# One row of a product order changed: the second set of unit 0 in a retention, MoE and Mish kernel

## The chip, the cores and the metric

The kernel runs on one core of one Trainium2 chip. What is measured is the device time of one execution in microseconds (us); three runs were taken of the kernel before the change. TensorE (PE) does the matrix products into PSUM, VectorE (DVE) and GpSimd (POOL) do elementwise work, ScalarE (ACT) copies and applies functions, SyncE (SP) issues most of the transfers. Each engine takes its instructions in the order in which the program hands them over, and an instruction that waits holds up everything behind it on that engine.

## The reference

Three layers in a row, on 2 x 576 = 1152 tokens of width 512:

```python
ret = scale * (q @ k.T) * Dmat          # 8 heads of 64, gamma ** (i - j) below the diagonal
x   = ret @ v                           # (1152, 512)
p   = probs / (probs.sum(-1) + 1e-9)
x   = sum over e of p[:, e] * (relu(x @ w1[e]) @ w2[e])    # 4 experts, 512 -> 1024 -> 512
h   = x @ w_in                          # 512 -> 2048
out = (h * tanh(softplus(h))) @ w_out   # 2048 -> 512
```

## The kernel before

The retention comes first (to about 37 us). Then come twelve *units* of 512 hidden columns: units 0 to 7 are the four experts (two units each), 8 to 11 the last layer. Every product is done with operands that are split into a high part, which ACT makes with a copy, and a low part, which is the rest and is made by a subtraction on DVE or POOL.

A unit's first layer, for 1024 of the tokens, is done in two *sets* of 256 hidden columns, written `("S", u, c)`. A set is a Strassen-like scheme: seven products, numbered 1 to 7, of six matmuls of 128x512 each, into four PSUM banks, one for each quarter of the result; a quarter is a token half t and a column half j. Products 1, 5, 7 and 6 open the banks of (t, j) = (0, 0), (1, 0), (0, 1) and (1, 1). Products 2, 3 and 4 add onto the banks of 1, 5 and 7. Before a bank is added onto, what it holds has to be kept: ACT copies products 1, 5 and 7 to the tiles p1, p5 and p7 (line 253).

`first_pair` (lines 639 to 694) writes the set out. `order` gives the products' order, `sum_at` the product behind which POOL adds p7 and p1 to p5. The lines that matter:

```python
                p16 = sum_tile("p16", ph); add(p16, done[n], p1)   # n == 6, L664-665
                    add(done[3], done[3], p16)          # n == 2, L669, only where 3 came earlier
            if n == sum_at:
                pool.tensor_tensor(out=p5, in0=p5, in1=p7, op=ALU.add)   # L673
                pool.tensor_tensor(out=p5, in0=p5, in1=p1, op=ALU.add)   # L674
            if n == 7:
                while later:
                    later.pop(0)()                      # weight work, handed over here
            ...
        add(done[6], done[6], p5)                       # after the last product
        hidden_high(*h6); hidden_low(*h4); hidden_low(*h6)   # h3 here too, where 3 was last
```

`add` runs on DVE (L645). The finished quarters are named after the products that end them: h2 is (0, 0), h3 (1, 0), h4 (0, 1) and h6 (1, 1). For each, `hidden_high` is the relu on ACT (L587) and `hidden_low` the low part on DVE (L596). The list `later` holds weight work: for the set ("S", 0, 1) these are two tasks, `task(pool, pool)`. The first splits the next unit's first weight chunk (ACT L175, then four subtractions on POOL, L179); the second is a set of four sums of weights on POOL (L139 to L142).

After the two sets of unit 0 the second layer begins: blocks `("Y", u, c, tb)`, 24 matmuls each (L753), for token half tb. The first block of unit 0 takes twelve matmuls with the hidden columns of set 0, then twelve with those of set 1: three with h2, three with h4, and again three and three. The first matmul of each three reads the low part. The second block reads the same hidden columns. Then comes the first set of unit 1.

Set 0 of unit 0 is written out another way (`first_plain`), since not all its operands exist yet. While it runs, DVE and ACT make the last of them: T3, T2 and T4 are differences (DVE L792) that are split (ACT L801, DVE L798). T4 is read by product 4 of the second set alone. The split's ACT copy for T4 is handed over ahead of the second set's copies p1, p5 and p7.

What the loop hands over for each set stands here:

Of the kernel before, what the change touches and what calls it, by code (L numbers as in the profile page):

```python
# [82 lines left out]
def retention_moe_mish(ctx: ExitStack, tc: tile.TileContext, kq_in, kv_in, probs, w1, w2, w64, cdec, out):  # L83
# [10 lines left out]
    order = [("O", 0, 0), ("O", 0, 1), ("G", 0, 1)]  # L94
# [97 lines left out]
    def weight_task(i, lo_engine, defer=False):  # L192
        if n_task[0] >= len(tasks):
            return
        sums, (m, u, c) = tasks[n_task[0]]
        raw = source.get(m, m), u, c
        if raw not in raw_t or not (sums or splits((m, u, c), i) and sums_at.get((m, u, c), -99) <= i - 1):
            return
        if sums:
            sums_at[m, u, c] = i  # L200
        n_task[0] += 1
        weight_sums((m, u, c)) if sums else split_w((m, u, c), lo_engine, defer)
# [14 lines left out]
    def split_x(out, src, lo_engine):  # L217
        act.activation(out=out[:, 0], in_=src, func=AF.Copy)
        lo_engine.tensor_tensor(out=out[:, 1], in0=src, in1=f32(out[:, 0]), op=ALU.subtract)
# [291 lines left out]
    def load64():  # L511
        i = n_ld[0]
        if i >= len(halves):
            return
        n_ld[0] += 1
        (m, u, c), half = halves[i]
        t = wraw.tile([P, 2, 256, 2], U32, tag="w64", name="w64", bufs=2)
        src = w64[0 if m == "O" else 1, u - NE, c, :, 2 * half:2 * half + 2]
        sp.dma_start(out=t, in_=src.bitcast(U32).rearrange("p k (n t) -> p k n t", t=2))
        raw64[i] = t  # L520
# [82 lines left out]
    def hidden(*args):  # L603
        hidden_high(*args)
        hidden_low(*args)

    def first_plain(u, c, behind):

        o = [[bank(t, j) for j in range(2)] for t in range(2)]
        h = [h_tile(u, c, i) for i in range(2)]  # L610
        for i, n in enumerate(PLAIN):
            t, j, opens = n[-3:]
            product(u, c, n, o)
            for f in behind.get(i, ()):
                f()
            if not opens:
                hidden(u, h[t][:, :, j], o[t][j])
# [94 lines left out]
    def first_last(u, c):  # L712

        o, w = ps_tile()[:, 0, :256], w_t["O", u, c]
        for k in range(4):
            for n, (a, b) in enumerate(((0, 1), (0, 0), (1, 0))):
                pe.matmul(o, xc[:, b, k], w[:, a, k], start=k == 0 and n == 0, stop=k == 3 and n == 2)  # L717
        turn_blocks(hs.rearrange("p k t -> p (k t)")[:, c * 256:(c + 1) * 256], o)
        if c == 1:
            turn_rest(hs)  # L720

    def first_last_both(u):

        n = [(2 * u + c) % 3 for c in range(2)]
        low, high = sorted(n)
        w = o_slots[:, low:high + 1:high - low]
        o = ps_tile()[:, 0]
        for k in range(4):
            for i, (a, b) in enumerate(((0, 1), (0, 0), (1, 0))):
                pe.matmul(  # L730
                    o.rearrange("p (c n) -> p c n", c=2), xc[:, b, k], w[:, :, a, k],
                    start=k == 0 and i == 0, stop=k == 3 and i == 2,
                )
        to = hs.rearrange("p k t -> p (k t)")
        if n[0] < n[1]:
            turn_blocks(to, o)
        else:
            for c in range(2):
                turn_blocks(to[:, c * 256:(c + 1) * 256], o[:, (1 - c) * 256:(2 - c) * 256])
        turn_rest(hs)  # L740
# [33 lines left out]
    def load_pb(e, tb):  # L774
        if e < E:
            pb = ph.tile([P, TB], F32, tag=f"pb{tb}", name="pb", bufs=1)
            row = p_dram[e:e + 1, tb * TB:(tb + 1) * TB]
            sp.dma_start(out=pb, in_=row.to_broadcast([P, TB]))
            pb_t[e, tb] = pb
# [5 lines left out]
    def t_first(n):  # L785
        out, x, y = {T1: (b11, b12, b11), T3: (b12, b22, b12), T2: (b11, b22, b11), T4: (b21, b21, b11)}[n]
        x_minus(out, x, y)
        hi(n, out)
        return lambda: lo(n, out)
# [174 lines left out]
    def feed_forward():  # L964
        for tb in range(NTB):
            load_pb(0, tb)
        rests = [t_first(T1), t_first(T3)]
        rests[0]()

        def first_t():  # L970
            rests.append(t_first(T2))
            rests[1]()


        sp.dma_start(out=p_last, in_=p_dram[:, NTB * TB:].rearrange("e t -> t e"))
        load64()
        load64()
        pbs = []
        i_x = seq.index(("Y", NE - 1, 0, 0))

        for i, (m, u, *at) in enumerate(seq):
            def task(*engines):
                for lo_engine in engines or (pool,):
                    weight_task(i, lo_engine)

            if m == "S":
                c, = at
                late = (u, c) in ((0, 0), (NE, 0))
                behind, order, sum_at = {}, (1, 5, 7, 6, 2, 4, 3), 7
                if (u, c) == (0, 0):  # L990
                    behind = {3: [first_t], 5: [lambda: first_last(u, 0)]}
                elif (u, c) == (0, 1):
                    behind = {1: rests[3:]}
                if (u, c) == (NE - 1, 1):
                    behind = {6: [lambda: first_last_both(u)]}
                if (u, c) == (NE, 0):
                    behind = {1: [lambda: split_x(xc, acc_last, pool)], 5: [last_x], 7: [last_t]}
                    behind[6] = [lambda: first_last(u, 0)]
                    order, sum_at = (1, 5, 7, 3, 6, 2, 4), 2
                elif (u, c) == (0, 1):  # L1000
                    later.append(lambda: task(pool, pool))
                elif (u, c) == (NE, 1):
                    later.append(lambda: task(pool, dve, dve))
                elif (u, c) == (NE + 1, 0):
                    later.append(task)
                elif c == 1:
                    later.append(lambda: task(*(pool,) * (2 if u == NE + 1 else 1)))
                if (u, c) == (0, 0):
                    first_plain(u, c, behind)
                    rests[2]()  # L1010
                    task(pool, pool)
                    rests.append(t_first(T4))
                else:
                    first_pair(u, c, behind, later, order, sum_at)
            elif m == "L":
                if u in (0, NE):
                    first_last(u, *at)
                elif at[0] == 1 and u != NE - 1:
                    first_last_both(u)
                if (u, *at) == (NU - 1, 0):  # L1020
                    for f in last_operands(u)[1:]:
                        f(T1)
            elif m == "T":
                m2_t(u)
            elif m == "V":
                last_second(u)
            else:
                if seq[i if u == NE - 1 else i - 1] == ("Y", u, 0, 0):
                    hidden(u, hl, hs)
                if i == i_x:  # L1030
                    task()
                m2(u, *at)
                if u < NE and u % 2 == 1 and at[0] == 1:
                    pbs.append((u // 2 + 1, at[1], i))

            ahead = i + 1 < len(seq) and seq[i + 1][0] == "S"

            catch_up = {("Y", 0, 0, 0): (dve, dve), ("L", 1, 0): (dve,), ("Y", 0, 0, 1): (pool, pool)}
            catch_up |= {("Y", NU - 2, 0, 1): (pool, pool)}
            catch_up |= {("Y", NE, 0, 0): (dve, pool), ("L", NE + 1, 0): (pool, pool)}  # L1040
            put_off = seq[i] in (("L", 0, 1), ("Y", NE, 0, 1), ("Y", NE, 1, 1))
            if m != "S" and i != i_x and not i_x + 2 <= i <= i_x + 4 and not put_off:
                task(*catch_up.get(seq[i], ()))
            if m != "S":
                new = (m, *at) in (("L", 0), ("L", 1), ("Y", 0, 0), ("Y", 0, 1)) and not i_x - 1 <= i <= i_x + 7 and i > 2
                turn64(new, later.append if ahead else lambda f: f())

            if not i_x <= i <= i_x + 1:
                load_w()
            if pbs and pbs[0][2] <= i - 2:  # L1050
                load_pb(*pbs.pop(0)[:2])

    feed_forward()


# [60 lines left out]
```

## Time and profile before

| What | us |
|---|---|
| Runs of the kernel before, median of 3 | 599.76 |
| Lowest and highest of them | 599.61, 599.93 |
| The profiled execution, its own time | 600.2 |
| Its span in the trace | 598.3 |
| TensorE busy in it | 590.7 (99%) |
| VectorE, GpSimd, ScalarE busy | 442.0, 394.0, 318.0 |

Busy shares are an average over stages with different limits; the stretch around the change is from 51 to 73 us, and the rows below are mostly from there. An idle time in brackets in a row is the time the engine stood still before that instruction, with what released it. A row with x8 stands for eight instructions, from the first one's start; its second number is the time from there to the last one's end.

### The profile page before, as it was taken

To read this page: it belongs to the slowest core of one execution; us is meant where nothing else is said; L and a number is where in the kernel's file an instruction comes from. 1 tells how busy PE (TensorE), PEld (TensorE's weight loads), DVE (VectorE), ACT (ScalarE), POOL (GpSimd) and SP (SyncE) were. 2 spreads that over 40 slices of the span, in tenths; PEclk is the share of its full clock that TensorE was granted. 3 is DMA by queue.
4 is the path that set the end of the run, shared out by engine and by line. 5 is a ranking of instruction groups with operands and counts; after the bars stand their busy time and mean duration, and the time that the engine had idled before them with its cause. 6 is when DMAs were issued, how large, how long until landed. Compare 5 with 4: busy or idle time off the path is not lost.

```text
span 598.3 us, 8362 instructions
## 1 busy us (share of the span) xinstructions
PE 590.7 (99%) x3069; PEld 491.7 (82%) x3069; DVE 442.0 (74%) x584; ACT 318.0 (53%) x485; POOL 394.0 (66%) x445
## 2 busy tenths in 40 slices
PE   8999999999999999999999999999999999999997
PEld 7888888888888888888888888888888888888886
DVE  4788678789779769869869859868767766245295
ACT  3566357456456455556546545425657755445360
POOL 2387759758748838847846856772787874853932
PEclk9999999999999999999999999999999999999999
DMA  8952306434623623631732632622222341220023
GB/s 326 397 184 75 109 15 192 142 89 147 188 89 94 206 88 89 213 121 53 211 121 74 220 100 86 176 80 61 56 85 88 125 124 70 71 70 1 0 72 123
DMA packets 57777, 72.29 MB, mean 121 GB/s; under 512 B 31240, under 2 KB 39048, under 8 KB 57736
## 3 DMA queue, kind: packets, MB, share of 16 engines
q1 hardware_dynamic: 57592, 71.46, 38.4%
q8 instruction: 24, 0.39, 0.3%
q10 hardware_dynamic: 144, 0.29, 0.2%
q14 instruction: 17, 0.14, 0.1%
HBM read 57.57 MB, written 14.17 MB: 120 GB/s over the span
## 4 chain that ended last, share of the span: by engine, by line
PE 90%; DMA 5%; POOL 2%; DVE 2%; ACT 1%; issue 1%; POOLq 0%; ACTq 0%; DVEq 0%; SPq 0%
PE ps L753 40%; PE b L242 38%; PE b L766 5%; PE ps L730 5%; DMA kq<-kq_in 3%; DMA cst_sb<-cdec 2%; PE ps L242 1%; POOL o L179 1%; DVE acc L792 1%; DVE x L798 1%; PE b L959 0%; PE ps L717 0%; DVE h L596 0%; ACT x L801 0%; POOL wr L142 0%
## 5 line engine op out<-in xcount | busy, mean ns | idle before, releaser
L753 PE MATMUL ps<-h,w 128*128 128x512 f32 x1056 | 243.2, 389 | 0.0
L753 PEld LDWEIGHTS ps<-h,w 128*128 128x128 f32 x1056 | 198.2, 188 | 41.4 <-DVE h L601 0.3
L179 POOL TENSOR_TENSOR w<-wr,w 128x256 fp32r<-128x256 f32 x180 | 148.0, 855 | 52.3 <-ACT w L175 52.3
L242 PE MATMUL b<-x,w 128*128 128x512 f32 x576 | 138.6, 390 | 0.0
L242 PEld LDWEIGHTS b<-x,w 128*128 128x128 f32 x576 | 107.6, 188 | 23.3 <-DVE acc L851 1.2
L179 POOL TENSOR_TENSOR o<-wr,o 128x256 fp32r<-128x256 f32 x92 | 80.4, 904 | 61.8 <-ACT o L175 61.8
L242 PE MATMUL b<-x,o 128*128 128x512 f32 x468 | 114.6, 390 | 0.6 <-ACT p L253 0.6
L242 PEld LDWEIGHTS b<-x,o 128*128 128x128 f32 x468 | 87.4, 188 | 19.3 <-ACT p L253 1.0
L645 DVE TENSOR_TENSOR b<-b,p 128x512 f32<-128x512 f32 x69 | 46.1, 695 | 34.9 <-PE b L242 32.4
L253 ACT ACTIVATE p<-b 128x512 f32<-128x512 f32 x69 | 40.4, 596 | 51.8 <-PE b L242 51.8
L175 ACT ACTIVATE w<-wr 128x1024 fp32r<-128x1024 f32 x48 | 50.3, 1054 | 28.5 <-POOL wr L142 20.6
L587 ACT ACTIVATE h<-b 128x512 fp32r<-128x512 f32 x64 | 37.8, 597 | 43.6 <-DVE b L645 32.3
L827 DVE TENSOR_TENSOR ps<-ps,pb 128x1024 f32<-128x1024 f32 x28 | 34.4, 1227 | 24.0 <-PE ps L753 24.0
L673 POOL TENSOR_TENSOR p<-p,p 128x512 f32<-128x512 f32 x23 | 33.5, 1458 | 20.5 <-ACT p L253 20.5
L540 ACT ACTIVATE e<-e,cbias 128x512 uint32<-128x512 uint32 x32 | 23.0, 718 | 42.3 <-DVE e L528 42.3
L596 DVE SCALAR_TENSOR_TENSOR h<-b,h 128x512 fp32r<-128x512 f32 x64 | 40.9, 681 | 0.0
L645 DVE TENSOR_TENSOR p<-b,p 128x512 f32<-128x512 f32 x23 | 15.8, 686 | 27.8 <-PE b L242 22.5
L551 DVE SCALAR_TENSOR_TENSOR g<-w,g 128x512 f32<-128x512 uint32 x32 | 35.9, 1123 | 0.0
L554 DVE TENSOR_TENSOR g<-g,e 128x512 f32<-128x512 f32 x32 | 34.4, 1075 | 1.1
L828 DVE TENSOR_TENSOR acc<-acc,ps 128x1024 f32<-128x1024 f32 x28 | 34.2, 1222 | 1.0
L674 POOL TENSOR_TENSOR p<-p,p 128x512 f32<-128x512 f32 x23 | 31.9, 1388 | 1.8
L766 PE MATMUL b<-w,hl 128*128 128x512 f32 x132 | 31.7, 389 | 0.0
(117 smaller groups left out, 700.1 us busy)
## 6 DMA issues: line engine op xcount, KB each, us to landing
wr<-w SPq DMA_DIRECT2D x32, 512.0 KB, 5.3
w<-w SPq DMA_DIRECT2D x32, 512.0 KB, 4.3
O<-g SPq DMA_DIRECT2D x16, 256.0 KB, 5.5
W<-g SPq DMA_DIRECT2D x16, 256.0 KB, 3.3
wr<-O SPq DMA_DIRECT2D x8, 512.0 KB, 3.8
wr<-W SPq DMA_DIRECT2D x8, 512.0 KB, 3.7
kq<-kq_in SPq DMA_DIRECT2D x7, 576.0 KB, 9.0
kv<-kv_in SPq DMA_DIRECT2D x7, 544.0 KB, 9.4
```

Source lines behind the costliest of these rows:

```text
L175: act.activation(out=w[:, 0], in_=t, func=AF.Copy)
L179: lo_engine.tensor_tensor(out=w[:, 1, k], in0=t[:, k], in1=f32(w[:, 0, k]), op=ALU.subtract)
L242: pe.matmul(o[t][j], w[:, a, 2 * kh + kk, fb * P:(fb + 1) * P], x[:, b, kk], start=opens and i == 0, stop=i == 5, skip_group_check=not opens,)
L253: act.activation(out=t, in_=src, func=AF.Copy)
L551: dve.scalar_tensor_tensor(out=g, in0=lo_w, scalar=2.0 ** -52, in1=g, op0=ALU.mult, op1=ALU.add)
L554: dve.tensor_tensor(out=g, in0=g, in1=e.bitcast(F32), op=ALU.mult)
L587: act.activation(out=out[:, 0], in_=src, func=AF.Relu)
L596: dve.scalar_tensor_tensor(out=out[:, 1], in0=src, scalar=0.0, in1=f32(out[:, 0]), op0=ALU.max, op1=ALU.subtract)
L645: dve.tensor_tensor(out=out, in0=a, in1=b, op=ALU.add)
L753: pe.matmul(o[:, j], w[:, a, d:d + P], h[:, b, f], start=i == f == n == 0, stop=i == f == 1 and n == 2,)
L766: pe.matmul(o, hl[:, a, 2 * k + f], w[:, b, f * DM:(f + 1) * DM], start=k == f == i == 0, stop=k == f == 1 and i == 2,)
L827: dve.tensor_tensor(out=o, in0=o, in1=pbb, op=ALU.mult)
```

## The change

One line is added: the second set of unit 0 gets the order 1, 5, 7, 3, 6, 2, 4 and the sums on POOL behind product 2, which only the first set of unit 8 had before. The order there was 1, 5, 7, 6, 2, 4, 3, with the sums behind product 7.

```diff
                 elif (u, c) == (0, 1):
                     behind = {1: rests[3:]}
+                    order, sum_at = (1, 5, 7, 3, 6, 2, 4), 2
                 if (u, c) == (NE - 1, 1):
```

It moves instructions on three engines. On TensorE, in the second set of unit 0, from product 7 to the second layer's first matmuls (b_804 is the bank of products 1 and 2, b_806 of 5 and 3, b_805 of 7 and 4, b_807 of 6):

```order
 L242 MATMUL b_805<-x,w 128x512 x6
+L242 MATMUL b_806<-x,w 128x512 x6
 L242 MATMUL b_807<-x,w 128x512 x6
 L242 MATMUL b_804<-x,o 128x512 x6
 L242 MATMUL b_805<-x,o 128x512 x6
-L242 MATMUL b_806<-x,w 128x512 x6
 L753 MATMUL ps<-h,w 128x512 x48
```

Product 3 has come forward from the end to the fourth place, and product 4 is now the last.

On POOL, at the same set (p_825 is p5, p_833 p7, p_816 p1; the rows on o are the first task of `later`, those on wr its second):

```order
+L179 TENSOR_TENSOR o<-wr,o 128x256 x4
+L139 TENSOR_TENSOR wr<-wr 128x2x128
+L140 TENSOR_TENSOR wr<-wr 128x2x128
+L141 TENSOR_TENSOR wr<-wr 128x2x128
+L142 TENSOR_TENSOR wr<-wr 128x2x128
 L673 TENSOR_TENSOR p_825<-p_825,p_833 128x512
 L674 TENSOR_TENSOR p_825<-p_825,p_816 128x512
-L179 TENSOR_TENSOR o<-wr,o 128x256 x4
-L139 TENSOR_TENSOR wr<-wr 128x2x128
-L140 TENSOR_TENSOR wr<-wr 128x2x128
-L141 TENSOR_TENSOR wr<-wr 128x2x128
-L142 TENSOR_TENSOR wr<-wr 128x2x128
```

The two sums into p5 now stand behind the eight instructions of the weight work, where they stood ahead of them.

On DVE, the end of the same set (p_852 and p_856 are p16; h<-b_805 is the low part of h4, h<-b_806 that of h3):

```order
-L645 TENSOR_TENSOR p_852<-b_807,p_816 128x512
-L645 TENSOR_TENSOR b_805<-b_805,p_852 128x512
+L645 TENSOR_TENSOR p_856<-b_807,p_816 128x512
+L645 TENSOR_TENSOR b_806<-b_806,p_856 128x512
 L596 SCALAR_TENSOR_TENSOR h<-b_804,h 128x512
-L645 TENSOR_TENSOR b_806<-b_806,p_852 128x512
+L645 TENSOR_TENSOR b_805<-b_805,p_856 128x512
+L596 SCALAR_TENSOR_TENSOR h<-b_806,h 128x512
 L645 TENSOR_TENSOR b_807<-b_807,p_825 128x512
 L596 SCALAR_TENSOR_TENSOR h<-b_805,h 128x512
-L596 SCALAR_TENSOR_TENSOR h<-b_806,h 128x512
 L596 SCALAR_TENSOR_TENSOR h<-b_807,h 128x512
```

The low part of h3 has moved ahead of the sum with p5 (b_807 and p_825); the low part of h4 stands right behind that sum in both. On ACT the relu of h3 now stands ahead of that of h4.

## Rows read from the trace of the kernel before

**Rows 1.** The page: busy time by engine, and the chain by engine.
```profile
PE 590.7 (99%) x3069; PEld 491.7 (82%) x3069; DVE 442.0 (74%) x584; ACT 318.0 (53%) x485; POOL 394.0 (66%) x445
...
PE 90%; DMA 5%; POOL 2%; DVE 2%; ACT 1%; issue 1%; POOLq 0%; ACTq 0%; DVEq 0%; SPq 0%
```

**Rows 2.** Chain of waits, 50 to 75 us: start, length, what.
```profile
54.56 1.69 DVE acc L792
56.25 0.02 issue
56.27 1.06 ACT x L801
57.34 0.49 ACT p L253
57.83 0.04 issue
57.87 4.37 PE b L242 x18
62.25 10.90 PE ps L753 x48
```

**Rows 3.** Timeline of TensorE: start, length, line, operation, tiles, count, idle before.
```profile
51.64 1.55 PE L242 MATMUL b<-x,o 128*128 128x512 f32 x6
53.03 4.24 PE L242 MATMUL b<-x,w 128*128 128x512 f32 x18
57.87 3.01 PE L242 MATMUL b<-x,o 128*128 128x512 f32 x12 [0.60 <-ACT p L253]
60.73 1.52 PE L242 MATMUL b<-x,w 128*128 128x512 f32 x6
62.08 11.06 PE L753 MATMUL ps<-h,w 128*128 128x512 f32 x48
72.98 1.52 PE L242 MATMUL b<-x,o 128*128 128x512 f32 x6
```

**Rows 4.** Timeline of ScalarE, around the three copies.
```profile
56.27 1.06 ACT L801 ACTIVATE x<-acc 128x1024 fp32r<-128x1024 f32 x1 [2.66 <-DVE acc L792]
57.24 1.55 ACT L253 ACTIVATE p<-b 128x512 f32<-128x512 f32 x3
58.67 1.07 ACT L175 ACTIVATE o<-wr 128x1024 fp32r<-128x1024 f32 x1
```

**Rows 5.** Line 253, 57.9 to 58.9 us: min/median/max ns, first and last start.
```profile
L253 ACT ACTIVATE p<-b x2: 590/595/600, 57.7 to 58.2; 128x512 f32<-128x512 f32 x2
```

**Rows 6.** Timeline of GpSimd, 52 to 75 us.
```profile
52.74 8.56 POOL L179 TENSOR_TENSOR w<-wr,w 128x256 fp32r<-128x256 f32 x8 [3.46 <-ACT w L175]
61.26 1.29 POOL L673 TENSOR_TENSOR p<-p,p 128x512 f32<-128x512 f32 x1
62.63 1.29 POOL L674 TENSOR_TENSOR p<-p,p 128x512 f32<-128x512 f32 x1
63.88 2.84 POOL L179 TENSOR_TENSOR o<-wr,o 128x256 fp32r<-128x256 f32 x4
66.80 0.74 POOL L139 TENSOR_TENSOR wr<-wr 128x256 f32<-128x256 f32 x1
...
69.24 0.74 POOL L142 TENSOR_TENSOR wr<-wr 128x256 f32<-128x256 f32 x1
73.55 0.85 POOL L139 TENSOR_TENSOR wr<-wr 128x256 f32<-128x256 f32 x1 [3.57 <-DVE o L179]
```

**Rows 7.** Timeline of VectorE, 63 to 73 us.
```profile
63.95 0.70 DVE L645 TENSOR_TENSOR b<-b,p 128x512 f32<-128x512 f32 x1 [0.97 <-POOL p L674]
64.56 1.88 DVE L596 SCALAR_TENSOR_TENSOR h<-b,h 128x512 fp32r<-128x512 f32 x3
67.75 1.23 DVE L825 TENSOR_TENSOR acc<-ps,pb 128x1024 f32<-128x1024 f32 x1 [1.31 <-PE ps L753]
71.11 1.22 DVE L179 TENSOR_TENSOR w<-wr,w 128x1024 fp32r<-128x1024 f32 x1 [2.14 <-ACT w L175]
```

**Rows 8.** Waits of TensorE's weight loads, 60 to 598 us: total, times, longest.
```profile
PEld b L242 <- DVE acc L851: 1.2, 6, 0.2
PEld ps L753 <- DVE h L601: 0.3, 1, 0.3
PEld b L242 <- POOL x L807: 0.3, 1, 0.3
```

**Rows 9.** GpSimd at its slower pace, from the timeline, 38 to 44 us.
```profile
38.06 1.07 POOL L139 TENSOR_TENSOR wr<-wr 128x256 f32<-128x256 f32 x1
...
41.70 1.60 POOL L142 TENSOR_TENSOR wr<-wr 128x256 f32<-128x256 f32 x1
```

**Rows 10.** VectorE beside it.
```profile
42.74 1.65 DVE L792 TENSOR_TENSOR acc<-acc 128x1024 f32<-128x1024 f32 x1
```

**Rows 11.** Weight loads at the program's start, and at 46 us, by line: min/median/max ns.
```profile
L434 PEld LDWEIGHTS ps<-zero x15: 288/330/333, 1.2 to 4.1; 128*128 128x128 f32 x15
...
L717 PEld LDWEIGHTS ps<-o,xc x12: 187/192/192, 45.8 to 47.2; 128*128 128x128 f32 x12
```

## The prediction

> **What bounds the kernel now.** I read the page first. TensorE is busy 99% of the span, and 90% of the chain that ended last is its own [rows 1]. So the time is TensorE's stream plus its pauses, and a change is worth what it adds to or takes from those pauses. Next came the list of its waits: from 60 us to the end the matmuls have none, and the weight loads three small groups, the longest wait 0.3 us [rows 8]. From 57.87 us on the chain is TensorE without a break [rows 2]. A pause that the change puts in after that is therefore paid in full: nothing later has slack to give it back.
>
> Then the stretch of the change. TensorE runs product 1 from 51.64 and products 5, 7 and 6 from 53.03; then it stands still for 0.60 us until ACT's copy [rows 3]. The chain says why. DVE ends the difference for T4 at 56.25, ACT splits it from 56.27 to about 57.3, and only then come the three copies p1, p5 and p7 [rows 2, 4]. Product 2 adds onto product 1's bank and needs p1; it starts at 57.87, when p1 is done. Products 2 and 4 (x12) and 3 (x6) follow, and the second layer starts at 62.08 [rows 3]. Its 48 matmuls take 10.90 us up to 72.98, which is 0.227 us each. After the pause, twelve matmuls took 60.73 - 57.87 = 2.86 instead of 12 x 0.227 = 2.72 us: a restart costs 0.14 us.
>
> At its end the set leans on POOL. POOL works off eight weight subtractions until 61.26, adds p7 and p1 to p5 by 63.92, and DVE, which had waited 0.97 us for that, starts its sum with p5 at 63.95 [rows 6, 7]. Behind it the low part of h4 starts at 64.56 and lasts 0.68 (the three take 1.88, with 0.08 of overlap each), so it ends at 65.24. The second layer wants it at its 16th matmul, 12 of set 0 and 3 of h2 having gone before: 62.08 + 15 x 0.227 = 65.49. That is a margin of 0.25 us, and no pause.
>
> **The change, part by part.** It adds no instruction and removes none.
>
> Product 3 in fourth place. It adds onto product 5's bank, so it waits for the copy p5, the second of the three. The last two copies start at 57.7 and 58.2, 0.59 us each [rows 5], so p5 is done at about 58.3. TensorE is through products 1, 5 and 7 at 53.03 + 12 x 0.227 = 55.75. The pause there is 58.34 - 55.75 = 2.6 us where it was 0.60, and four products instead of three lie behind it: 58.34 + 0.14 + 24 x 0.227 = 63.93 for the second layer's start, against 62.08. Taken alone this step costs +1.85 us. Nothing ahead of the copies on ACT or DVE is moved, so I see no way for them to come sooner.
>
> The sums on POOL behind the weight work. The eight instructions for the weights wait for nothing new: ACT's split for them ends at 59.74 [rows 4]. So POOL starts them at 61.26, and does the same ten instructions in another order, in 66.80 - 61.26 plus four sums up to 69.98, in all 8.72 us [rows 6]. p5 is whole at 69.98 instead of 63.92. On DVE the sum with p5 starts at 70.01; the low part of h4 starts 0.61 later (64.56 - 63.95) and lasts 0.68: 71.30.
>
> The two together. TensorE starts the second layer at 63.93 and reaches the 16th matmul at 63.93 + 3.41 = 67.34. The low part of h2 is there by then: its bank is ready at 62.5, and it wants one relu and one subtraction, 0.6 and 0.68. But that of h4 is not: TensorE waits until 71.33, about 4.0 us. The first pause is thus swallowed: what sets the end is POOL's 69.98, whenever the second layer began. After the wait, 0.14 for the restart and 33 matmuls: 71.33 + 0.14 + 33 x 0.227 = 78.96. The next set then begins at 78.96 instead of 72.98: +5.98 us.
>
> What moves with it. The weight work is done 2.6 us earlier, at 67.36, but ACT's next splits stand behind the relu of h6, which waits for the same sum on DVE, and DVE's subtraction L179 (71.11 before) stands behind L825. L825 now waits for the first block, 78.96 - 24 x 0.227 = 73.5; so L179 ends near 73.5 + 1.23 + 1.22 = 76. The set of unit 1 wants it with its second product, 78.96 + 1.36 = 80.3: 4 us to spare. POOL's next sums wait for DVE (3.57 us idle before them in row 73.55 [rows 6]) and come some 3.5 us later, less than TensorE's own 6. SP's order is the same, and the transfers that these tasks free come at most 3.5 us later in a program that runs 6 us later. Those terms are nothing.
>
> The low parts of h3 and h6 are read only by the blocks of the second token half, behind the set of unit 1: nothing.
>
> So: +6.0 us. The profiled execution took 600.2, its span 598.3 and 1.9 around it, which would become 606.2. It lies 0.44 above the median of the runs; against that median I forecast 599.76 + 6.0 = 605.8.
>
> **Bounds of the pace on POOL.** The price is the time of the eight weight instructions. In the trace they run at 0.71 us (2.84 / 4) and 0.81 us each ((69.24 - 66.80) / 3), beside DVE work that has one input in PSUM [rows 6, 7]; after the change they would run beside the same kind. Nearby, beside a DVE subtraction with both inputs in SBUF, the same four sums took 41.70 + 1.60 - 38.06 = 5.24 instead of 3.18 us [rows 9, 10]. So the ends are +5.98 and +5.98 + 2.06 = +8.0 for the sums; a gain is excluded, since the ten instructions are all on POOL's one queue ahead of the sum. I take the fast end: from 67 to 70 us DVE has nothing to do but wait. The Trainium skill ("GPSIMD Engine Reference", Key points) says that GpSimd shares its SBUF interfaces with VectorE and suffers from DVE instructions with two SBUF inputs; the rows agree, and by it the fast pace holds, +6.0, since DVE's work there has an input in PSUM.
>
> **Rivals.**
>
> (a) TensorE's clock falls in the wait. No pause of the matmuls here is as long as 4 us, so the trace doesn't exclude it. At the program's start, after standing idle, the weight loads took 330 ns, later 192 [rows 11], which looks like the lower of the two levels, 1.2 against 2.4 GHz. That stretch is 15 loads long, from 1.2 to 4.1 plus 0.33. If the wait costs such a stretch, 3.2 x (1 - 192 / 330) = 1.4 us are lost, up to half of it, 1.6, if everything runs at half pace: +7.4 to +7.6, 607.2 to 607.4. For it speaks the start; against it that the array is at work right up to the wait. The Trainium skill ("TensorE: Matmul & The Clock Gate", HAM oscillation) warns that waits in the middle of a kernel send the clock back to half and that each such return is paid again; by that rule this case, not mine, would be the outcome.
>
> (b) POOL runs at the slow pace: up to +8.0, 607.8. It decides if DVE works SBUF to SBUF from 61 to 70; it does not in the order.
>
> (c) Only the first pause counts: +1.85, 601.6. That would be so if the low part of h4 did not need the sum with p5 to pass first. But they stand in one queue on DVE, the sum ahead.
>
> (d) Not slower: the delay is given back later. If TensorE's even pace hid waits for operands, everything behind would be readier after a late start and TensorE would run faster from 79 us on, back to 599.8 or less. It decides if 6.0 of the 520 us behind it, 1.2%, are such waits. Against it: the 48 matmuls take 10.90 us at 62 us, just behind the critical weights, and rows 8 hold 1.8 us in all.
>
> **How the numbers follow.** My case 66%: 605.4 to 606.4. (a) 22%, (b) 5%, (c) 4%, (d) 3%. The range from 605.1 to 607.9 takes in my case, (a) and most of (b). A measurement of this kernel tells 0.2%, 1.2 us, from no change. Slower by more than that: mine, (a), (b) and (c), 97%; within it: 2%, faster 1%, both out of (d).
>
> **What would show it.** In the profile after: TensorE idle about 2.6 us ahead of its fourth product, released by the copy L253; POOL's L673 near 67.4; DVE's sum L645 released by L674 near 70; TensorE idle about 4 us inside the 48 matmuls of L753, released by L596; the next set at about 79. I am wrong if that second wait is missing, if its matmuls behind are slower than 0.227 us apart, or if the next set begins at 79 and the time is not 6 us up.

## The result, and the profile after

| | before, us | after, us |
|---|---|---|
| Median of the runs (4 each) | 599.68 | 606.64 |
| Lowest and highest | 599.23, 599.93 | 604.61, 606.77 |
| Profiled execution, its span | 600.2, 598.3 | 606.68, 604.8 |

The ratio is 1.0109, with a 95% interval from 1.0087 to 1.0131: slower by 5.2 to 7.9 us. The forecast was 605.8, in a range from 605.1 to 607.9. A fourth run of the kernel before, 599.23, stands beside the three that the forecast started from.

TensorE around the change, in the timeline of the changed kernel (start, length, line, operation, count, idle before), against [rows 3]:

```profile
53.66 2.88 PE L242 MATMUL b<-x,w 128*128 128x512 f32 x12
58.28 3.01 PE L242 MATMUL b<-x,w 128*128 128x512 f32 x12 [1.74 <-ACT p L253]
61.13 2.88 PE L242 MATMUL b<-x,o 128*128 128x512 f32 x12
63.85 3.56 PE L753 MATMUL ps<-h,w 128*128 128x512 f32 x15
71.21 9.39 PE L753 MATMUL ps<-h,w 128*128 128x512 f32 x33 [3.80 <-DVE h L596]
80.44 1.52 PE L242 MATMUL b<-x,o 128*128 128x512 f32 x6
```

Two pauses stand where there was one of 0.60. The first is ahead of the fourth product, released by ACT's copies, the second behind exactly 15 matmuls of the second layer, released by DVE's low part. The next set starts 7.46 us later than before (80.44 against 72.98).

What released the second pause is read on GpSimd, against [rows 6] (same columns):

```profile
61.17 2.83 POOL L179 TENSOR_TENSOR o<-wr,o 128x256 fp32r<-128x256 f32 x4
...
67.23 1.26 POOL L673 TENSOR_TENSOR p<-p,p 128x512 f32<-128x512 f32 x1
68.57 1.26 POOL L674 TENSOR_TENSOR p<-p,p 128x512 f32<-128x512 f32 x1
```

and on VectorE, against [rows 7]:

```profile
69.87 0.70 DVE L645 TENSOR_TENSOR b<-b,p 128x512 f32<-128x512 f32 x1 [4.53 <-POOL p L674]
70.48 1.45 DVE L596 SCALAR_TENSOR_TENSOR h<-b,h 128x512 fp32r<-128x512 f32 x2
```

GpSimd's sum ends at 69.83, VectorE takes it at 69.87 after 4.53 us of standing still, the low part of h4 follows, and TensorE goes on at 71.21. The chain of waits of the changed kernel stands on GpSimd from 52.66 to 69.84 us: the eight subtractions that came ahead of the weight work are on the path as well.

One thing is not in those rows: the 33 matmuls behind the wait. By TensorE's starts they took 80.44 - 71.21 = 9.23 us, where 33 x 0.227 and a restart would be 7.63. The stretches say why (stretch, its length, TensorE's busy time and instructions, granted clock, DMA share, GB/s):

```profile
68.00:72.00 4.00, 0.79 (x3) 1.00 0.00 0
72.00:73.00 1.00, 1.00 (x4) 0.65 0.00 0
73.00:75.00 2.00, 2.00 (x6) 0.50 0.00 0
75.00:76.00 1.00, 1.00 (x4) 0.65 0.00 0
76.00:80.00 4.00, 4.00 (x20) 1.00 0.40 127
```

The granted clock is 1.00 through the wait, 0.50 from 73 to 75, and whole again from 76: TensorE was on the lower of its two levels, 1.2 GHz, for much of the stretch from 72 to 76, after it had gone back to work. The difference is 9.23 - 7.63 = 1.60 us. That the clock is its cause is shown by e9 below, where the wait is filled.

Of the 7.46 us the span shows 6.5, since the program's end came out shorter. The last work on the chain, before:

```profile
593.85 0.42 DVE acc L889
```

and after:

```profile
601.18 0.42 DVE acc L889
```

It ends at 594.27 and 601.60, 7.33 us apart; behind it lay 4.0 us to the end of the span before, and 3.2 after. Nothing of the change stands there, and in the other executions profiled that stretch is between 2.9 us (e10) and 4.0 us (e2) long: it varies from execution to execution, whatever the change.

### The profile page after: what moved, and what is told of

It is laid out like the page before. It is cut to its first block, busy times and chain, and to the rows that moved or that the text cites. A ratio compares the mean times of both kernels' runs of the same rounds, so it can differ in the third digit from the quotient of the medians.

```text
span 604.8 us, 8360 instructions
## 1 busy us (share of the span) xinstructions
PE 593.7 (98%) x3069; PEld 494.1 (82%) x3069; DVE 444.6 (74%) x584; ACT 318.5 (53%) x485; POOL 393.3 (65%) x445
## 4 chain that ended last, share of the span: by engine, by line
PE 90%; POOL 5%; DMA 2%; issue 2%; DVE 0%; SPq 0%; POOLq 0%
PE ps L753 39%; PE b L242 37%; PE b L766 5%; PE ps L730 5%; POOL w L179 2%; DMA kq<-kq_in 1%; POOL o L179 1%; PE ps L242 1%; DMA kv<-kv_in 1%; PE ps L400 1%; PE b L959 0%; PE ps L717 0%; PE b L366 0%; PE ps L385 0%; POOL wr L142 0%
## 5 line engine op out<-in xcount | busy, mean ns | idle before, releaser
L179 POOL TENSOR_TENSOR w<-wr,w 128x256 fp32r<-128x256 f32 x180 | 146.4, 846 | 51.4 <-ACT w L175 51.4
L673 POOL TENSOR_TENSOR p<-p,p 128x512 f32<-128x512 f32 x23 | 33.4, 1453 | 25.0 <-ACT p L253 25.0
```

The source lines that it names most:

```text
L179: lo_engine.tensor_tensor(out=w[:, 1, k], in0=t[:, k], in1=f32(w[:, 0, k]), op=ALU.subtract)
```

## The experiments

The theory: what sets the end is GpSimd's sum into p5, wherever TensorE stands by then; the longer pause on the copy p5 is swallowed by the wait for that sum; and the lower clock behind the wait comes on top. The rival: the new product order itself costs the time.

| Kernel | Median, us | Before beside it | Ratio, 95% interval |
|---|---|---|---|
| e1, order alone | 602.45 | 599.47 | 1.0047 (1.0034 to 1.0059) |
| e2, place of the sums alone | 607.56 | 599.47 | 1.0133 (1.0120 to 1.0147) |
| e3, changed, 15 matmuls in the wait | 606.14 | 599.47 | 1.0109 (1.0096 to 1.0123) |
| e4, sums between the two weight tasks | 602.22 | 599.47 | 1.0053 (1.0039 to 1.0067) |
| e6, old order, T4 late, sums first | 598.87 | 599.90 | 0.9986 (0.9976 to 0.9996) |
| e7, new order, T4 late | 598.39 | 599.90 | 0.9975 (0.9965 to 0.9984) |
| e8, changed, T4 late | 607.12 | 599.90 | 1.0116 (1.0100 to 1.0131) |
| e9, e8 with 28 matmuls in the wait | 604.81 | 599.90 | 1.0076 (1.0064 to 1.0089) |
| e10, e7 with the sums first | 598.01 | 599.59 | 0.9975 (0.9964 to 0.9986) |

**The order alone (e1)**, against the changed kernel:

```diff
-                    order, sum_at = (1, 5, 7, 3, 6, 2, 4), 2
+                    order, sum_at = (1, 5, 7, 3, 6, 2, 4), 7
```

> The new product order, with the sums on POOL back behind product 7. Theory (POOL's late sum sets the end, the order costs only the longer pause on the copy p5): the pause ahead of product 3 stays, 1.7 to 2.6 us, the second layer starts near 63.85 instead of 62.08, and no wait follows inside its 48 matmuls, so +1.8 us, 601.5. Rival (the order itself costs the 7 us): 606.6.

Measured: 602.45, and 600.71 in the profiled execution, whose TensorE timeline is this:

```profile
52.85 2.88 PE L242 MATMUL b<-x,w 128*128 128x512 f32 x12
57.95 3.02 PE L242 MATMUL b<-x,w 128*128 128x512 f32 x12 [2.21 <-ACT p L253]
60.80 2.88 PE L242 MATMUL b<-x,o 128*128 128x512 f32 x12
63.52 11.04 PE L753 MATMUL ps<-h,w 128*128 128x512 f32 x48
74.40 1.52 PE L242 MATMUL b<-x,o 128*128 128x512 f32 x6
```

The pause on the copy is there, the wait in the second layer is not, and the next set starts 1.4 us late (74.40 against 72.98). So the order does not cost the 7 us. The other four runs took 602.2 to 603.1, at a mean granted clock of 0.997 where the profiled one had 1.00. The expected 601.5 lies between; where those four lost the clock no trace of them shows. That it was behind this same pause, as in e3 below, is likely and not shown.

**The place of the sums alone (e2)**:

```diff
-                    order, sum_at = (1, 5, 7, 3, 6, 2, 4), 2
+                    sum_at = 2
```

> The old product order, with the sums on POOL behind product 2, so behind the weight work. Theory: the second layer starts at 62.08 as before, then waits from 65.5 to 71.2 for the low part of h4, 5.7 us, +5.9 us in all, and the matmuls behind the wait run at the lower clock, 1.7 to 1.9 us more: 607.3. Theory without the clock: 605.6. Rival (the order itself costs): 599.7, no change.

Measured: 607.56. The rows of TensorE behind the set:

```profile
61.41 3.56 PE L753 MATMUL ps<-h,w 128*128 128x512 f32 x15
70.60 10.68 PE L753 MATMUL ps<-h,w 128*128 128x512 f32 x33 [5.63 <-DVE h L596]
81.11 1.52 PE L242 MATMUL b<-x,o 128*128 128x512 f32 x6
```

The old order, a second layer that starts when it used to, and all of the loss: the wait is 5.63 us instead of 3.80. The sums' place is the cause, and the order adds nothing to it. The 33 matmuls behind the wait took 81.11 - 70.60 = 10.51 us, 2.88 more than 7.63, at a granted clock of 0.50 from 70 to 76 us.

**Between the two weight tasks (e4)**, new order:

```diff
                 while later:
                     later.pop(0)()
+                    if sum_at == 8 and len(later) == 1:
+                        pool.tensor_tensor(out=p5, in0=p5, in1=p7, op=ALU.add)
+                        pool.tensor_tensor(out=p5, in0=p5, in1=p1, op=ALU.add)
 ...
-                    later.append(lambda: task(pool, pool))
+                    later.extend([task, task])
```

(with `sum_at = 8` in the row of the order.)

> The new product order, with the sums on POOL between the two weight tasks, behind four instructions instead of eight. Theory (the time follows POOL's sum): the sum ends at 66.7 instead of 69.8, the low part of h4 at 68.0, TensorE waits 0.8 us instead of 3.8, and the clock stays: 599.7 + 1.8 + 0.9 = 602.4. Rival (any place behind weight work costs the whole): 606.6. Rival (the sum's place does not matter): 601.5 as with the order alone.

Measured: 602.22, against 602.4. The wait in the second layer shrinks with GpSimd's end (L680 is here the second of the two sums):

```profile
65.49 1.29 POOL L680 TENSOR_TENSOR p<-p,p 128x512 f32<-128x512 f32 x1
68.15 7.77 PE L756 MATMUL ps<-h,w 128*128 128x512 f32 x33 [0.56 <-DVE h L596]
75.76 1.52 PE L242 MATMUL b<-x,o 128*128 128x512 f32 x6
```

The sum ends at 66.78 instead of 69.83. Four instructions ahead of the sums instead of eight take 3.2 us off the wait, and the 33 matmuls take their usual time (75.76 - 68.15 = 7.61 to the next set).

**Matmuls in the wait (e3)**, changed kernel, in the second layer's first block:

```diff
+                    if (u, c, tb, i, j, f) == (0, 0, 0, 1, 0, 1):
+                        fill = bank(0, 0)
+                        for _ in range(15):
+                            pe.matmul(fill, rows(u, 0)[:, 0, :P], h_t[u, 0, tb][:, 0, 0], start=True, stop=True)
```

> The changed kernel with 15 matmuls of 128x512 put into TensorE's long wait, into a bank that nobody reads (work added, none left out). Theory (the clock falls because TensorE stands idle, and that costs about 1.8 us): 15 x 0.227 = 3.4 us of the 3.8 are filled, the clock is granted in full at 72 to 76 us, the 33 matmuls behind take 7.5 us, and the time is 606.6 - 1.8 = 604.8. Rival (the 33 matmuls are slow because of the traffic of ACT and DVE beside them): unchanged, 606.6. Rival (the added matmuls cost their own time): 610.

Measured: 606.14, which by itself settles nothing; the one run whose mean clock was 1.00 took 605.08, near the expected 604.8. The profiled one, 606.31, shows what went wrong. TensorE:

```profile
58.44 4.46 PE L242 MATMUL b<-x,w 128*128 128x512 f32 x12 [2.58 <-ACT p L253]
62.74 2.89 PE L242 MATMUL b<-x,o 128*128 128x512 f32 x12
65.47 3.56 PE L757 MATMUL ps<-h,w 128*128 128x512 f32 x15
68.87 3.56 PE L755 MATMUL b<-h,w 128*128 128x512 f32 x15
72.27 7.64 PE L757 MATMUL ps<-h,w 128*128 128x512 f32 x33
79.75 1.52 PE L242 MATMUL b<-x,o 128*128 128x512 f32 x6
```

and its granted clock (columns as above):

```profile
58.00:59.00 1.00, 0.56 (x1) 0.58 0.81 120
59.00:61.00 2.00, 2.00 (x6) 0.50 0.30 44
61.00:62.00 1.00, 1.00 (x4) 0.72 0.40 83
```

Here the clock fell behind the *first* pause, of 2.58 us, and the second layer started at 65.47 instead of 63.85. The added matmuls then ran past the point where the low part was ready, about 71.3, and cost almost 1 us themselves. Still, the 33 matmuls behind took 79.75 - 72.27 = 7.48 us, with ACT and DVE as busy beside them: that traffic does not slow them.

**No first pause (e8), and the same with the wait filled (e9)**. ACT's copy for T4 is handed over behind the three copies; e9 has e3's lines too, with 28 matmuls. The cuts from the edit stand in the order in which the program reaches them:

```diff
-                    rests.append(t_first(T4))
+                    x_minus(b21, b21, b11)
 ...
-                    behind = {1: rests[3:]}
+                    behind = {7: [lambda: lo(T4, b21)]}
 ...
+                    later.append(lambda: hi(T4, b21))
                     later.append(lambda: task(pool, pool))
```

> The changed kernel with T4's copy behind p1, p5 and p7, so without its first pause. Theory (what sets the end is POOL's sum at 69.8, and the first pause is swallowed by the second): TensorE starts the second layer 2.5 us sooner and waits 6.4 instead of 3.8 us, the end is where it was, and the clock falls as in the run with the sums alone: 607.0 to 608.0. Rival (the two pauses add up): 606.6 - 1.8 = 604.8 or less.

> The same, with 28 matmuls of 128x512 in the long wait, into a bank that nobody reads (work added, none left out). Theory (above the wait itself, what the changed kernel loses is TensorE's clock): no pause is long enough to lower the clock in any run, 28 x 0.227 = 6.4 us of the wait are filled, and all runs come out at 599.5 + 5.7 = 605.2, with the clock at 1.00 from 66 to 80 us. Rival (the clock falls in the first stretch anyway, or the loss is not the clock): 606.5 to 607.5.

Measured: 607.12 and 604.81. TensorE in e8, then its clock:

```profile
60.79 3.56 PE L753 MATMUL ps<-h,w 128*128 128x512 f32 x15
70.88 10.41 PE L753 MATMUL ps<-h,w 128*128 128x512 f32 x33 [6.52 <-DVE h L596]
81.13 1.52 PE L242 MATMUL b<-x,o 128*128 128x512 f32 x6
```

```profile
68.00:70.00 2.00, 0.00 (x0) 0.91 0.00 0
70.00:71.00 1.00, 0.12 (x1) 0.50 0.00 0
71.00:76.00 5.00, 5.00 (x12) 0.50 0.00 0
76.00:77.00 1.00, 1.00 (x4) 0.77 0.00 0
```

TensorE in e9:

```profile
63.90 6.51 PE L755 MATMUL b<-h,w 128*128 128x512 f32 x28
70.49 7.77 PE L757 MATMUL ps<-h,w 128*128 128x512 f32 x33
78.11 1.52 PE L242 MATMUL b<-x,o 128*128 128x512 f32 x6
```

In e8 the first pause is gone, the second layer starts 3.1 us sooner than in the changed kernel, and the program is no faster: the first pause had been swallowed whole. All its runs have a mean clock of 0.994. In e9 TensorE is kept busy through the same wait; the 33 matmuls take 78.11 - 70.49 = 7.62 us instead of 10.25 (81.13 - 70.88), and the program takes 2.3 us less with 28 matmuls more. That is the clock's price for a wait of 6.5 us. What is left, 604.81 - 599.90 = 4.9 us, is under the 5.7 expected; but the kernel before has the pause of 0.60 us, which e9 has not. Against e7 below, which has the same edit and no long wait, it is 604.81 - 598.39 = 6.4 us, the length of the wait. One run of e9 (605.18) still had a mean clock of 0.997.

**Versions without the waits (e6, e7, e10).** All three have e8's edit. e7 is the new order with the sums behind product 7; e6 the old order with this, and e10 the new order with this:

```diff
-                    task(pool, pool)
+                    task()
 ...
-                    later.append(lambda: task(pool, pool))
+                    later.append(lambda: task(pool, pool, pool))
```

which hands one of the two weight splits that stood ahead of the sums over behind them.

> The new product order with the sums on POOL behind product 7, and T4's copy behind p1, p5 and p7. Theory (the order costs nothing but the wait for a copy that stands behind T4's): no pause ahead of product 3, the second layer starts near 61.3; POOL's sum ends at 63.9 as before, so a wait of about 0.5 us in the second layer: 599.4, and no lower clock in any run, where the order alone took 602.45. Rival (product 3 in fourth place is late for another reason): 601 to 602.5.

> The kernel before, with ACT's split copy for T4 handed over behind the copies p1, p5 and p7 (T4 is read by product 4 alone), and the second of POOL's two weight splits handed over behind the two sums into p5. Theory: the pause of 0.6 us goes with its restart, the second layer starts near 61.3, the sums on POOL are done near 60, no wait follows: 599.5 - 0.7 = 598.8. Rival (the pause only moves, to T4 or to the weight split that comes later): 599.5 or more.

> The new product order with T4's copy behind p1, p5 and p7, the sums into p5 behind product 7, and the second of POOL's two weight splits behind those sums. Theory (what is left of waits in the version without that last step is 0.44 us on POOL's sum, plus the restart): POOL's sum is done near 60.6, product 4 comes last and finds T4's low part ready, TensorE runs from 52 to 72 us without a wait: 598.4 - 0.5 = 597.9, against 599.5 to 599.9 of the kernel before. Rival (the weight split that now ends near 63.5 comes too late for the second layer): 598.4 or more.

Measured: 598.39, 598.87 and 598.01, all faster than the kernel before. e7 on TensorE:

```profile
52.44 5.60 PE L242 MATMUL b<-x,w 128*128 128x512 f32 x24
57.88 2.88 PE L242 MATMUL b<-x,o 128*128 128x512 f32 x12
60.60 3.56 PE L753 MATMUL ps<-h,w 128*128 128x512 f32 x15
64.60 7.77 PE L753 MATMUL ps<-h,w 128*128 128x512 f32 x33 [0.44 <-DVE h L596]
72.21 1.52 PE L242 MATMUL b<-x,o 128*128 128x512 f32 x6
```

Products 5, 7, 3 and 6 run without a stop. The new order costs nothing once the copies come in time; with T4's product last, it even leaves T4 more time. The time is 1.0 us under the expected 599.4. Of the 1.9 us between the profiled executions of the kernel before and of e7, 0.77 are there at the next set (72.21 against 72.98), and 1.0 lie behind the last work on the chain, 3.0 us against 4.0; how the median came to gain 1.5 us is not shown beyond that. In e6, where product 4 is not the last, a wait shows that was not expected:

```profile
59.54 0.73 PE L242 MATMUL b<-x,o 128*128 128x512 f32 x2 [0.37 <-DVE x L798]
```

and DVE's subtraction for T4 beside it is slow, 2.33 us where it was 1.24:

```profile
57.16 2.33 DVE L798 TENSOR_TENSOR x<-acc,x 128x1024 fp32r<-128x1024 f32 x1 [0.95 <-ACT x L801]
```

It runs beside GpSimd's second sum, which the same step has brought forward to 58.48 and which takes 2.15 us there instead of 1.29. In e10 product 4 comes later and that wait is gone:

```profile
53.06 5.60 PE L242 MATMUL b<-x,w 128*128 128x512 f32 x24
58.50 2.88 PE L242 MATMUL b<-x,o 128*128 128x512 f32 x12
61.22 11.04 PE L753 MATMUL ps<-h,w 128*128 128x512 f32 x48
```

Whether e10 is faster than e7 is not settled: they were timed apart, and their ratios to the kernel before are the same, 0.9975.

## Why the prediction was right or wrong, point by point

**Right: where the time would go.** TensorE's stream with its pauses set the time, and no delay was given back in the 520 us behind it: 7.46 us at the next set, 7.33 at the last work on the chain. Rival (d) is out; the 0.8 us that the span got back lie behind that last work.

**Right: GpSimd's queue.** Forecast were L673 near 67.4, the sum whole at 69.98, DVE's sum at 70.01, TensorE on at 71.33; the trace has 67.23, 69.83, 69.87 and 71.21. The fast pace held, so rival (b) is out. e2 and e4 show it as the cause, from two sides: the wait grows or shrinks with the place of the sums.

**Right in kind, off in size: the first pause.** The copy came as forecast (58.28 against 58.34), but TensorE came later, with product 5 at 53.66 instead of 53.03, so the pause was 1.74 instead of 2.6. In the executions of e1, e3 and e4, which hand over the same up to there, product 5 starts at 52.85, 52.97 and 53.11, and the pause is 2.21, 2.58 and 2.46: the stretch ahead varies by more than half a microsecond. It did not matter, because the pause is swallowed, as e8 shows.

**Wrong: the clock.** The step that failed is "after the wait, 0.14 for the restart and 33 matmuls", priced at 0.227 us each, and with it the 66% for a clock that stays. They took 9.23 / 33 = 0.280 us each, which the prediction itself had named as a sign of being wrong. Rival (a), given 22%, is what happened, at 1.60 us in the profiled execution where 1.4 to 1.6 were worked out from the weight loads at the program's start. That reading of [rows 11] holds: from 73 to 75 us, where 0.50 is granted, the weight loads took 330 ns again. (Over the program's start itself the profile's clock row reads 1.00, so there the level is not shown by that row.) e9 shows that it is the standing still that costs: filled, the same wait leaves 7.62 us for the 33 matmuls. The argument against (a), that the array works right up to the wait, did not hold. The Trainium skill ("TensorE: Matmul & The Clock Gate", HAM oscillation) warns that a wait in the middle of a kernel puts the clock back to half. The trace agrees, with 0.50 granted from 73 to 75 us.

So 605.8 came as near to 606.64 as it did in part by luck, with a term of 1.6 us missing. Without the lower clock the next set would have started at 71.21 + 7.63 = 78.84 against a forecast of 78.96, so up to there the rest of the sum came out. But the stretch behind the last work was 0.8 us shorter than in the profiled execution before, which hid half of the missing term. The time lies above the 605.4 to 606.4 of the prediction's own case and below the 607.2 to 607.4 of rival (a). Why one of the four runs took 604.61, at a mean clock like that of the others, stays open: no trace of it was taken.

Rival (c), that only the first pause counts, did not happen in the changed kernel; e1 shows it in kind, for the order alone.

## What to carry to other kernels

When an instruction is handed over at another point, look at what is already in line on its engine there: two sums of 1.3 us moved behind 6 us of work that had no hurry, and a matrix engine waited for them. Two waits on one path do not add up when the second is for something that comes in its own time; only the last release counts, so taking the first wait away (e8) bought nothing. And price a wait of a few microseconds on TensorE at more than its length: the clock behind it is part of the bill.

## What the runs showed of the hardware that was not expected

The granted clock can fall after the work has been resumed: in the changed kernel it was 1.00 through the wait from 67.4 to 71.2 and 0.50 from 73 to 75. In e8 and e2 it was at 0.50 from 70 us on, before the matmuls went on at 70.88 and 70.60.

Behind a pause of 2.58 us (e3) the clock fell; behind 2.46 (e4), 2.21 (e1) and 1.74 (the changed kernel) it did not. These are single executions, and whether the length of the pause alone decides is not shown. Nor does the price simply grow with the wait: it was 1.60 us behind 3.80, 2.88 behind 5.63 (e2) and 10.25 - 7.63 = 2.62 behind 6.52 (e8), in one execution each.
